# Filter spectra of four chunks kept in SBUF over the end of a stage, and stored later from another queue

## The chip, the cores and the metric

The kernel runs on one core of one Trainium2 chip (trn2). The metric is the device time of one execution in microseconds, the median over several executions. The engines are TensorE (PE, with PEld for its weight loads), VectorE (DVE), ScalarE (ACT) and GpSimd (POOL). SyncE (SP) issues most of the DMAs and ACT some of them. The 16 DMA engines carry both queues.

## What is computed

A long convolution by FFT, gated by its input, and then an MLP with two matrices, over 2 batches of 12480 tokens of 128 values:

```python
h_filt = (np.maximum(pos_emb @ w1, 0.0) @ w2) * window
u = x * v
Uf = np.fft.rfft(u, n=L, axis=1)
Hf = np.fft.rfft(h_filt, n=L, axis=0)
y = np.fft.irfft(Uf * Hf[None, :, :], n=L, axis=1)[:, :S, :]
attn_out = x * y
h = attn_out.reshape(B * S, D) @ w_in
out = np.maximum(0.01 * h, h) @ w_out
```

The filter's spectrum `Hf` is the same for both batches.

## The kernel before

**Stages.** The transforms are done as matrix products. In the first stage, 16 chunks of rows of batch 0 are loaded, multiplied (`x*v`), transformed and stored to DRAM (`scr1`), together with the filter's rows. The second stage (the loop over `ORD`, from line 823) takes 25 chunks of 4 frequencies. Of each it makes the filter's spectrum `hs` (PE line 846, ACT copies line 850), the input's spectrum `up` (line 135), their complex product on DVE and POOL (`product`, lines 143 and 144), and the way back `dp` (line 163), which ACT copies to `ct` (line 238). After the stage tile 0 of batch 0 is joined and gated (`front0`), and then the MLP runs in blocks of up to 512 tokens with 16 steps each (`m1`, `m2`, lines 1009 and 1050 to 1052). It is fed by `front(t)` for tiles of 390 tokens, and batch 1's convolution (`conv`) is done in pieces between the MLP's steps.

**What is stored.** `hspec` in DRAM holds the filter's spectrum for batch 1: `store_h` (line 809) issues two DMAs of 256 KB for each chunk on ACT's queue. Batch 1 reads it back at line 489, some 250 us later. `ct` goes to `scr2`, one chunk behind, also from ACT's queue (`store_back`, line 220). The weights' conversion (`weights`, lines 708 to 762) is spread over the same loop: DVE turns 64-bit data into 32-bit, in eight parts whose loads (lines 717, 718) SP issues.

**Order.** Each engine executes its instructions in the order in which the program writes them, and waits only by semaphores. The SP queue in the loop holds, in this order: the chunk three ahead (`load_b`, line 705), parts of tile 0's upper rows (`first_c`), in chunks 20 and 23 a whole input chunk of batch 1's first stage (`fetch_a`: one load of `ft` and six of `x` and `v`), in chunks 23 and 24 the gating data of tiles 0 and 1 (`load_gx`). Behind the loop come the last rows of tile 0 (`last_c`, line 657), the last `store_back`, the rows of tile 1 (`upper_c(1)` and `rows_c`, lines 629 to 650), and the loads of tile 2. In the MLP a list of steps (`at(i, what, t)`, carried out by `do`) says at which step a load is issued or a piece done. Step 2 has "piece" (stores held back and the third `fetch_a`), step 6 the loads of tile 3 ("loadc"), step 9 the third product `mult_a` on POOL and tile 3's gating data ("loadg"), steps 13 and 14 tile 4's loads, steps 16 to 23 the sums of tile 3 on POOL (`join_hi`, `join_lo`: tiles `cq` and `cp`), step 25 the transform of tile 3 on PE (`yp`, line 932). Batch 1's chunk 2 issues the fourth `fetch_a` at its beginning, and between its two halves the fourth `mult_a` stands in POOL's queue, ahead of the last `cp` of tile 3.

**Buffers.** `fetch_a` takes its three tiles from pool `s0`, tags `s0` (3 buffers), `s1` (3) and `s2` (2), in rotation. The two first fetches are made in the second stage, the third at MLP step 2. The results `o1` of batch 1's first stage rotate over two buffers of tag `s4` in pool `sc`. `hs` has two buffers of its own. The first `next(conv)`, which stands ahead of the loop, runs only to the first `yield`: it takes the first `o1` buffer and issues nothing.

Of the kernel before, what the change touches and what calls it, by code (L numbers as in the profile page):

```python
# [8 lines left out]
F32 = mybir.dt.float32  # L9
# [12 lines left out]
MC1 = 4  # L22
KC = 4
# [7 lines left out]
def tile_conv_mlp(ctx, tc, x, v, pos_emb, w1, w2, w_in, w_out, cf, cr, cg, cb, ci, cw, out):  # L31
# [210 lines left out]
    with tc.manual_schedule():  # L242
# [175 lines left out]
        wc_l = wp.tile([128, D], F32R, name="wc_l")  # L418
        sc = ctx.enter_context(tc.tile_pool(name="sc", bufs=2, reuse_waits="tile"))
        psc = {}  # L420
        N1 = HB // MC1
        WAIT = 12
        PRE = 2
# [273 lines left out]
        with ExitStack() as st:  # L697
# [97 lines left out]
            def evac(c):  # L795
# [10 lines left out]
                    last_c(ct, k0, n, [nc.sync] * 3 + [nc.scalar if end else nc.sync])  # L806
                store_back(0, c, ct, nc.sync if end else nc.scalar)

            def store_h(c, hs, i):

                w = chunk(c)[1] * D

                def put(eng):
                    for s in range(2):
                        eng.dma_start(out=hspec[c][:, :, s, :w], in_=hs[HB * s:HB * s + HB, :, :w])
                put(nc.scalar)

            eh, dps = {}, {}
            first_c = upper_c(0)
            ahead(A0)  # L820
            next(conv)
            hidden(ORD[0])
            for i, c in enumerate(ORD):
                if i + 3 < NCH:
# [18 lines left out]
                for ri in range(2):  # L843
                    for k in range(n):
                        h, j = 64 * (k % 2), ri * n // 2 + k // 2
                        nc.tensor.matmul(hp[k % 2][:, D * j:D * j + D], es[h:h + 64, k // 2, ri, :], w22[h:h + 64, :],
                                         start=True, stop=True)
                hs = sbb.tile([128, 2, KC // 2, 2, D], F32, tag="hs", name="hs", bufs=2)
                for k in range(2):
                    nc.scalar.copy(hs[:, :, :n // 2, k, :],  # L850
                                   hp[k][:, :n * D].rearrange("p (r j d) -> p r j d", r=2, d=D))
# [28 lines left out]
            back_halves(dps[ORD[-1]], pins.pop(ORD[-1]), ORD[-1])  # L880
            evac(ORD[-1])
            run(join_hi(0))
            run(upper_c(1))
            rows_c(1, 0, 0, KH)
            psc["held"] = []
# [278 lines left out]
                at(0, "load", t)  # L1164

        at(2, "piece", 0)
        at(9, "mult", PRE)

        def do(what, t, i):
            if what == "piece":  # L1170
                run(pieces_out.pop(0))
                for f in psc.pop("held"):
                    f()
                fetch_a(PRE)
            elif what == "mult":
                mult_a(t)
            elif what == "conv":
                run(conv)
                load_tile(t)
                load_tile(t + 1)  # L1180
            elif what == "load":
                if t not in ld:
                    load_tile(t)
            elif what == "loadc":
                load_c(t)
            elif what == "loadg":
                load_gx(t)
            elif what == "join":
                run(join(t))
            elif what == "sum":  # L1190
                if t not in joins:
                    joins[t] = join(t)
                next(joins[t])
            elif t in fronts:
                next(fronts[t], None)
            else:
                fronts[t] = front(t, i // NF)
                next(fronts[t])
# [118 lines left out]
```

## Time and profile before

| | us |
|---|---|
| median of 3 runs | 1598.55 |
| lowest, highest | 1595.64, 1606.63 |
| profiled execution | 1601.6 |
| its span, first to last instruction | 1599.7 |
| PE busy | 1555.3 (97%) |
| DVE, ACT, POOL busy | 1138.7, 998.1, 767.0 |

The page's table of 40 slices of 40 us each gives the stages: the first up to about 140 us, the second up to about 315, then the MLP. The DMA engines are busy for eight tenths and more up to 280 us, mostly for five to seven tenths up to some 960 us, where batch 1's convolution runs beside the MLP, and for two tenths or less at the end. The granted TensorE clock is 0.996 of full speed over the span (full speed is 2.4 GHz, the lower level 1.2 GHz). In the rows below each engine's line says when an instruction began, how long it took, and in brackets how long the engine had idled ahead of it and what ended that. A line with "x2" is two instructions merged. SPq and ACTq are DMA issues and other queue instructions; their time is that of the issue, not of the transfer.

### The profile page before, as it was taken

What the parts mean: (1) busy time and instruction counts of PE and PEld (TensorE: products, weight loads), DVE (VectorE), ACT (ScalarE), POOL (GpSimd) and SP (SyncE); (2) the same over time, 40 slices, a digit from 0 to 9 for tenths busy, and PEclk for the clock granted to TensorE, in tenths of its full rate; (3) what the DMA queues carried; (4) which work ended last, traced back from release to release, by engine and by line L of the source; (5) the groups of instructions that cost most, each with busy time, mean ns of one, the idle gap of its engine ahead of it and who ended that gap; (6) DMA issues with size and microseconds to landing.
All of it is one profiled execution on the core that took longest, in us unless ns stands there. A gap on an engine that the chain in (4) does not pass through costs nothing.

```text
span 1599.7 us, 27485 instructions
## 1 busy us (share of the span) xinstructions
PE 1555.3 (97%) x9241; PEld 1322.6 (83%) x9241; DVE 1138.7 (71%) x1785; ACT 998.1 (62%) x2108; POOL 767.0 (48%) x806
## 2 busy tenths in 40 slices
PE   7888999899999999999999999999999999999998
PEld 7887555588889888888888888988888888888888
DVE  6874888756975566666676765677777777777776
ACT  2332555346664477777777776667777676777776
POOL 6772122146654275867776873633443433334310
PEclk9999999999999999999999999999999999999999
DMA  9998999767767477657556650421212212121200
GB/s 268 304 307 283 320 318 340 243 198 203 222 198 216 136 194 192 197 162 197 173 160 181 171 153 32 138 85 55 69 54 68 80 57 89 56 61 59 64 11 21
DMA packets 166268, 253.30 MB, mean 158 GB/s; under 512 B 14240, under 2 KB 118932, under 8 KB 163056
## 3 DMA queue, kind: packets, MB, share of 16 engines
q1 hardware_dynamic: 146388, 226.28, 47.7%
q10 hardware_dynamic: 19740, 25.28, 4.5%
q8 instruction: 73, 1.20, 0.3%
q14 instruction: 67, 0.55, 0.1%
HBM read 168.03 MB, written 83.43 MB: 157 GB/s over the span
## 4 chain that ended last, share of the span: by engine, by line
PE 75%; DMA 11%; DVE 8%; ACT 2%; issue 2%; POOL 1%; SPq 1%; ACTq 0%; DVEq 0%; POOLq 0%
PE mh L1009 29%; PE acc L1051 9%; PE acc L1052 9%; PE acc L1050 9%; PE yp L932 4%; PE cv L149 3%; DMA scr<-o 3%; PE cv L445 3%; DMA scr<-ct 2%; DMA ft<-in_cf_dram 2%; PE op L1082 2%; PE a L398 2%; PE zp L951 1%; PE up L135 1%; DVE ta L143 1%
## 5 line engine op out<-in xcount | busy, mean ns | idle before, releaser
L1014 DVE SCALAR_TENSOR_TENSOR rl<-mh,rh 128x512 fp32r<-128x512 f32 (+1 forms) x336 | 226.7, 682 | 198.7 <-ACT rh L1013 197.4
L1022 DVE TENSOR_TENSOR rl<-mh,rh 128x512 fp32r<-128x512 f32 (+2 forms) x416 | 277.4, 670 | 83.6 <-ACT rh L1021 75.1
L1017 ACT ACTIVATE mh<-mh 128x512 f32<-128x512 f32 (+2 forms) x416 | 236.9, 570 | 153.8 <-PE mh L1009 143.5
L1009 PE MATMUL mh<-zh,w_in_h 128*128 128x512 f32 (+3 forms) x800 | 315.9, 395 | 3.8 <-DVE rl L1014 2.6
L1009 PE MATMUL mh<-zl,w_in_h 128*128 128x512 f32 (+3 forms) x800 | 299.2, 374 | 0.3 <-POOL zl L965 0.2
L1051 PE MATMUL acc<-rl,w_out_h 128*128 128x512 f32 (+3 forms) x800 | 299.1, 374 | 0.1
L1050 PE MATMUL acc<-rh,w_out_h 128*128 128x512 f32 (+3 forms) x800 | 299.0, 374 | 0.0
L1052 PE MATMUL acc<-rh,w_out_l 128*128 128x512 f32 (+3 forms) x800 | 299.0, 374 | 0.0
L1009 PE MATMUL mh<-zh,w_in_l 128*128 128x512 f32 (+3 forms) x800 | 299.0, 374 | 0.0
L1013 ACT ACTIVATE rh<-mh 128x512 fp32r<-128x512 f32 (+1 forms) x336 | 199.1, 596 | 136.8 <-PE mh L1009 128.4
L965 POOL TENSOR_TENSOR zl<-zf,zh 128x390 fp32r<-128x390 f32 (+24 forms) x110 | 67.7, 628 | 395.7 <-ACT zh L964 371.0
L687 POOL TENSOR_TENSOR cp<-cq,cp 98x256 f32<-98x256 f32 x248 | 194.1, 783 | 29.3 <-DVE cp L675 12.6
L1019 DVE CAST rh<-mh 128x512 fp32r<-128x512 f32 (+2 forms) x208 | 139.5, 671 | 65.6 <-ACT mh L1017 65.3
L1009 PEld LDWEIGHTS mh<-zh,w_in_h 128*128 128x128 f32 x800 | 151.2, 189 | 30.1 <-DVE rl L1014 9.2
L1051 PEld LDWEIGHTS acc<-rl,w_out_h 128*128 128x128 f32 x800 | 151.2, 189 | 20.2 <-DVE rl L1022 0.4
L1050 PEld LDWEIGHTS acc<-rh,w_out_h 128*128 128x128 f32 x800 | 151.2, 189 | 19.8
L1052 PEld LDWEIGHTS acc<-rh,w_out_l 128*128 128x128 f32 x800 | 151.2, 189 | 19.7
L1009 PEld LDWEIGHTS mh<-zh,w_in_l 128*128 128x128 f32 x800 | 151.2, 189 | 19.7
L1009 PEld LDWEIGHTS mh<-zl,w_in_h 128*128 128x128 f32 x800 | 151.6, 190 | 15.9 <-POOL zl L965 0.6
L1021 ACT CAST rh<-mh 128x512 fp32r<-128x512 f32 (+2 forms) x208 | 118.7, 571 | 6.7
L684 POOL TENSOR_TENSOR cq<-cin 98x256 f32<-98x256 f32 x124 | 97.3, 784 | 0.9 <-DMA cin<-scr 0.8
L144 POOL TENSOR_TENSOR pin<-ta,tb 128x512 f32<-128x512 f32 (+1 forms) x23 | 28.8, 1253 | 130.7 <-DVE tb L143 130.7
(168 smaller groups left out, 2559.3 us busy)
## 6 DMA issues: line engine op xcount, KB each, us to landing
cin<-scr SPq DMA_DIRECT2D x318, 98.0 KB
hd<-hspec SPq DMA_DIRECT2D x48, 512.0 KB
bin<-scr SPq DMA_DIRECT2D x24, 768.0 KB
scr<-o SPq DMA_DIRECT2D x28, 588.0 KB
scr<-ct SPq DMA_DIRECT2D x25, 512.0 KB
scr1b<-o SPq DMA_DIRECT2D x32, 392.0 KB
hspec<-hs ACTq DMA_DIRECT2D x48, 256.0 KB
xm<-in_x_dram SPq DMA_DIRECT2D x128, 96.0 KB
```

Of the source, the lines that this page charges most:

```text
L684: eng.tensor_tensor(out=cq[:, p], in0=ci_t[:, 0, :, 0, :], in1=ci_t[:, 0, :, 1, :], op=op)
L687: eng.tensor_tensor(out=cp[:, p, w], in0=cq[:, p], in1=cp[:, p, 1], op=op)
L1009: nc.tensor.matmul(hp, u[:, fs], m, start=(i == 0), stop=(i == 2))
L1013: nc.scalar.activation(out=split2(rh), in_=plain(hp), func=AF.Relu)
L1014: nc.vector.scalar_tensor_tensor(out=split2(rl), in0=plain(hp), scalar=0.0, in1=split2(rh), op0=ALU.max, op1=ALU.subtract)
L1017: nc.scalar.activation(out=hp, in_=hp, func=AF.Lrelu, alpha=0.01)
L1019: nc.vector.tensor_copy(split2(rh), plain(hp))
L1021: nc.scalar.copy(split2(rh), plain(hp))
L1022: nc.vector.tensor_tensor(out=split2(rl), in0=plain(hp), in1=split2(rh), op=ALU.subtract)
L1050: nc.tensor.matmul(ap, w_out_h[:, f, :], rh, start=(f == 0 and not sums(k)), stop=False)
L1051: nc.tensor.matmul(ap, w_out_h[:, f, :], rl, start=False, stop=False)
L1052: nc.tensor.matmul(ap, w_out_l[:, f, :], rh, start=False, stop=(f == NF - 1))
```

## The change

For the chunks at places 19 to 22 of the order, `hs` is not written to its own two buffers but to other ones: two share one buffer of tag `s4`, one takes a buffer of tag `s1`, one of tag `s0`. The stores to `hspec` are not issued in the loop from ACT but kept as functions that issue them from SP: the first two (four DMAs) behind the stage ahead of tile 1's loads, the third and fourth (two DMAs each) at MLP steps 6 and 7, where step 6 already has the loads of tile 3 ahead of it. The first `next(conv)` moves from ahead of the loop to chunk 19, behind the allocation of the shared buffer, so that this buffer comes first in the rotation and the first `o1` second. What is computed is the same.

```diff
--- before.py
+++ after.py
@@ -418,6 +418,7 @@
         wc_l = wp.tile([128, D], F32R, name="wc_l")
         sc = ctx.enter_context(tc.tile_pool(name="sc", bufs=2, reuse_waits="tile"))
         psc = {}
+        kept = []
         N1 = HB // MC1
         WAIT = 12
         PRE = 2
@@ -806,6 +807,25 @@
                     last_c(ct, k0, n, [nc.sync] * 3 + [nc.scalar if end else nc.sync])
                 store_back(0, c, ct, nc.sync if end else nc.scalar)
 
+            KEEP = range(NCH - 6, NCH - 2)
+            pair = []
+
+            def place_h(i):
+
+                j = i - KEEP[0]
+                if i not in KEEP:
+                    return sbb.tile([128, 2, KC // 2, 2, D], F32, tag="hs", name="hs", bufs=2)
+                if j < 2:
+                    if j == 0:
+                        pair.append(sc.tile([128, 2048], F32, tag="s4", name="hs2"))
+                        next(conv)
+                    t = pair[0][:, 1024 * j:1024 * j + 1024]
+                elif j == 2:
+                    t = s0.tile([128, 1024], F32, tag="s1", name="hs1", bufs=3)
+                else:
+                    t = s0.tile([128, MC1 * 4 * NA], F32, tag="s0", name="hs0", bufs=3)[:, :1024]
+                return t.rearrange("p (r j i d) -> p r j i d", r=2, j=KC // 2, d=D)
+
             def store_h(c, hs, i):
 
                 w = chunk(c)[1] * D
@@ -813,12 +833,13 @@
                 def put(eng):
                     for s in range(2):
                         eng.dma_start(out=hspec[c][:, :, s, :w], in_=hs[HB * s:HB * s + HB, :, :w])
-                put(nc.scalar)
+                if i in KEEP:
+                    kept.append(lambda: put(nc.sync))
+                else:
+                    put(nc.scalar)
 
             eh, dps = {}, {}
             first_c = upper_c(0)
-            ahead(A0)
-            next(conv)
             hidden(ORD[0])
             for i, c in enumerate(ORD):
                 if i + 3 < NCH:
@@ -845,7 +866,7 @@
                         h, j = 64 * (k % 2), ri * n // 2 + k // 2
                         nc.tensor.matmul(hp[k % 2][:, D * j:D * j + D], es[h:h + 64, k // 2, ri, :], w22[h:h + 64, :],
                                          start=True, stop=True)
-                hs = sbb.tile([128, 2, KC // 2, 2, D], F32, tag="hs", name="hs", bufs=2)
+                hs = place_h(i)
                 for k in range(2):
                     nc.scalar.copy(hs[:, :, :n // 2, k, :],
                                    hp[k][:, :n * D].rearrange("p (r j d) -> p r j d", r=2, d=D))
@@ -880,6 +901,8 @@
             back_halves(dps[ORD[-1]], pins.pop(ORD[-1]), ORD[-1])
             evac(ORD[-1])
             run(join_hi(0))
+            for f in kept[:2]:
+                f()
             run(upper_c(1))
             rows_c(1, 0, 0, KH)
             psc["held"] = []
@@ -1164,6 +1187,8 @@
                 at(0, "load", t)
 
         at(2, "piece", 0)
+        at(6, "kept", 2)
+        at(7, "kept", 3)
         at(9, "mult", PRE)
 
         def do(what, t, i):
@@ -1172,6 +1197,8 @@
                 for f in psc.pop("held"):
                     f()
                 fetch_a(PRE)
+            elif what == "kept":
+                kept[t]()
             elif what == "mult":
                 mult_a(t)
             elif what == "conv":
```

## Rows read from the trace of the kernel before

**Rows 1.** Chain of waits, middle of the stage: start us, us, engine, tile, line

```profile
186.57 0.69 DVE ta L143
...
192.30 0.68 DVE ta L143
...
198.40 0.68 DVE ta L143
...
204.81 0.68 DVE ta L143
```

**Rows 2.** Windows: us, busy (instructions) by engine, then PEclk, DMA share, GB/s

```profile
core 0: us, PE busy (x) PEld busy (x) DVE busy (x) ACT busy (x) POOL busy (x), PEclk, DMA share, GB/s
264.00:270.00 6.00, 6.00 (x52) 3.51 (x52) 5.58 (x13) 2.53 (x6) 1.28 (x1) 1.00 1.01 351
295.00:300.00 5.00, 5.00 (x28) 2.33 (x30) 4.76 (x8) 2.35 (x5) 3.36 (x2) 0.70 0.96 291
318.00:324.00 6.00, 4.64 (x35) 3.02 (x34) 3.95 (x12) 0.69 (x4) 1.46 (x2) 1.00 0.54 177
```

**Rows 3.** Chain of waits, end of the stage

```profile
281.40 8.61 DMA scr<-ct
```

**Rows 4.** Timeline of ACT, end of the stage

```profile
291.73 1.07 ACT L850 COPY hs<-hp 128x512 f32<-128x512 f32 x2 [5.41 <-DVE fb L90]
...
303.90 1.07 ACT L238 COPY ct<-dp 128x512 f32<-128x512 f32 x2 [4.04 <-DMA hspec<-hs]
```

**Rows 5.** Timeline of DVE, the first product of chunks 19, 21, 22 and 23

```profile
270.52 0.68 DVE L143 TENSOR_TENSOR ta<-up,hs 128x512 f32<-128x512 f32 x1
...
284.03 0.69 DVE L143 TENSOR_TENSOR ta<-up,hs 128x512 f32<-128x512 f32 x1 [0.42 <-ACT hs L850]
...
292.90 0.69 DVE L143 TENSOR_TENSOR ta<-up,hs 128x512 f32<-128x512 f32 x1 [1.14 <-ACT hs L850]
...
301.46 0.68 DVE L143 TENSOR_TENSOR ta<-up,hs 128x512 f32<-128x512 f32 x1
```

**Rows 6.** Line 734 from 255 us (ns min/median/max), and POOL beside its last

```profile
L734 DVE TENSOR_TENSOR w_in_l<-wi,w_in_h x3: 411/426/2383, 255.5 to 296.3; 128x256 fp32r<-128x256 f32 x3
...
295.56 2.80 POOL L262 TENSOR_TENSOR xv<-xv,xv 98x1024 f32<-98x1024 f32 x1
```

**Rows 7.** Issues of hspec's stores and loads: ns min/median/max, first and last start

```profile
L815 ACTq DMA_DIRECT2D hspec<-hs x50: 515/516/1186, 156.6 to 308.1; - x50
L489 SPq DMA_DIRECT2D hd<-hspec x50: 451/578/610, 558.0 to 953.1; - x50
```

**Rows 8.** Timeline of PE and DVE, the MLP's first steps

```profile
323.10 0.43 PE L1009 MATMUL mh<-zh,w_in_h 128*128 128x390 f32 x1 [0.70 <-ACT zh L996]
...
326.31 0.42 DVE L684 TENSOR_TENSOR cq<-cin 98x256 f32<-98x256 f32 x1
...
327.18 0.69 DVE L100 TENSOR_TENSOR o<-cv,a1s 98x512 f32<-98x512 f32 x1
```

**Rows 9.** Timeline of SP: tile 1's first loads, and the fourth fetch's first

```profile
316.93 1.48 SPq L629 DMA_DIRECT2D cin<-scr  x3
...
350.88 0.33 SPq L249 DMA_DIRECT2D ft<-in_cf_dram  x1
```

**Rows 10.** Waits of SP, 240 to 345: us in total, times, longest

```profile
SPq L650 <- DMA cin<-scr: 1.3, 2, 1.1
```

**Rows 11.** Timelines of POOL and PE around tile 3's transform

```profile
359.20 2.36 POOL L262 TENSOR_TENSOR xv<-xv,xv 98x1024 f32<-98x1024 f32 x1 [9.61 <-DMA xv<-in_v_dram]
361.51 0.74 POOL L687 TENSOR_TENSOR cp<-cq,cp 98x256 f32<-98x256 f32 x1
...
362.80 1.10 PE L932 MATMUL yp<-cp,gt 98*64 98x128 f32 x16
```

**Rows 12.** Timeline of PE in the stage, after two stops

```profile
293.35 1.16 PE L846 MATMUL hp<-w,es 64*128 64x128 f32 x16 [2.55 <-ACT es L793]
294.93 3.44 PE L135 MATMUL up<-bin,mb 128*64 128x512 f32 x8 [0.42 <-DVE ta L143]
...
304.22 1.94 PE L135 MATMUL up<-bin,mb 128*64 128x512 f32 x8 [1.59 <-DVE ta L143]
```

## The prediction, made before the result

> **What bounds the kernel now.** I read the page first (engines and slices), then the chain of waits from 140 to 420 us, then three timelines (ACT, SP, DVE) around the place that the diff touches. From the page the reader takes that PE is busy 97% of the span, and that all but a short early part is the MLP: what is won ahead of the MLP is worth its full size, and what is lost in it too. The change sits at the end of batch 0's second stage and in the first MLP blocks, so only 260 to 370 us need a close look.
>
> The stage has two limits that nearly coincide. DVE: in the undisturbed middle, the first product instruction of every third chunk comes 18.24 us later [rows 1], that is 6.08 us a chunk, in steps of 5.73, 6.10 and 6.41 us that repeat. DMA: the windows show a busy share of 1.01 at 351 GB/s shortly before the end of the stage [rows 2], so a chunk's traffic fills its time. At chunk 20 the loop adds seven loads for the first conversion chunk of batch 1, at chunk 23 seven more, and there the DMA side gives way. The chain leaves the engines and runs along a `ct` store of 8.61 us [rows 3]. The reader is to see in ACT's timeline what that costs: ACT issues these stores itself, and an issue is held until an earlier transfer has landed, so the copies behind it stand. `hs` of chunk 22 is written after 5.41 us of idling, `ct` of chunk 22 after 4.04 us that the trace puts down to a `hspec` store [rows 4].
>
> How much of this reaches the end is read from DVE, which does the products in order [rows 5]. From chunk 19 at 270.52, the undisturbed steps would put chunk 20 at 276.93 (+6.41), 21 at 282.66 (+5.73), 22 at 288.76 (+6.10). The last two come at 284.03 and 292.90: 1.4 and 4.1 us late, and both wait for ACT's `hs`. From 22 to 23 it takes 8.56 instead of 6.41, but that is not the DMAs: one `w_in_l` of 2.38 us, where its median is 0.43 [rows 6], runs beside POOL's 2.80 us product of the next stage, 1.96 us of the 2.15. So the DMA congestion costs the stage **4.1 us**, and some 0.2 more behind.
>
> **The change part by part.**
> *Eight stores leave ACT's queue* (chunks 19 to 22, two each of 256 KB). Issue time is 0.52 us each [rows 7], 1.0 us a chunk on ACT, which is not what holds DVE when nothing is blocked: nothing. What counts is 8 x 262 kB = 2.1 MB out of the crowded window: at 351 GB/s, 6.0 us of transfer time. The loads of chunk 20 and the weights that DVE converts then land earlier, and the waits of `hs` for its two-buffer ring (chunk 21 for the stores of 19, 22 for 20, 23 for 21) are gone. Bounds: below, nothing, if the loads fill the freed time; above, the 4.3 us, and 2 x 1.96 more if both POOL products (the second follows in the tail) came to lie beside instructions that they do not hold. Since 6.0 us of relief is more than the 4.1 us of lag, and the late products waited for just these copies, I take **-4.1 us**.
> *`next(conv)` moves to chunk 19*: it only allocates, it issues nothing on any queue. Nothing. The pair's buffer then goes to the second `o1`, first written by DVE at 327.18 [rows 8]; the two stores from it are issued some 8 us earlier. Hidden; if they landed later, DVE and all `rl` behind it would stand.
> *The two idle `s0`/`s1` buffers*: the third `fetch_a` now takes chunk 0's buffers and the fourth the kept ones. Chunk 0 is read before the MLP begins, and between the kept stores and the fourth fetch SP issues all of tile 4's loads. Nothing.
> *Four store issues on SP behind the last `store_back`.* SP issues a transfer of this shape in 0.58 us (the loads of `hspec` [rows 7]), so 2.1 to 2.3 us stand ahead of the seven `cin` loads of tile 1, which start at 316.93 now [rows 9]. Cover: SP itself waits up to 1.1 us for an earlier transfer ahead of the last two of these loads [rows 10], the DMA share is 0.54 there [rows 2], and DVE's `cq`, which needs them, starts at 326.31 [rows 8], over 5 us after the last issue. I take nothing for `cq`, and a shift of 1.0 to 2.3 us for everything behind on SP.
> *Four more at steps 6 and 7.* They stand behind tile 3's `cin` loads and ahead of tile 3's and 4's remaining loads and of the fourth `fetch_a`, which SP issues from 350.88 [rows 9]: again 2.1 to 2.3 us. From here nothing is free. SP goes from load to load, and the fourth fetch is awaited: POOL idles 9.61 us for it, multiplies 359.20 to 361.56, then does the last `cp` of tile 3 until 362.25, and PE transforms tile 3 at 362.80 [rows 11]. The slack is at most 0.55 us. A later fetch makes a later `mult_a(3)`, a later `cp`, and a PE that stands, with all MLP matmuls behind it.
> So SP is late by 2.1 us (the first four absorbed) to 4.6 (none absorbed). I take 3.1, the first four costing 1.0 net of the wait that they fill. Less 0.4 of slack: **+2.7 us** of idle PE; below, zero, if the fetch were not bound by its issue; above 4.6.
> *The clock.* After 2.55 us of idle PE the matmuls `up` took 3.44 us; after 1.59 us of idle they took 1.94 [rows 12], and the granted clock in that first stretch is 0.70 [rows 2], so part of it ran at the lower level (1.2 GHz). In the stage this hid behind DVE. In the MLP PE is the bound, and a stop of 2.7 us is nearer the first row: 3.44 - 1.94 = **+1.5 us**; zero if the stop stays under some 1.6 us.
> Sum: -4.1 + 2.7 + 1.5 = +0.1 us, on the profiled execution's span of 1599.7 us (1601.6 around it, 1.9 us outside). The median of the runs shown is 1598.55; the same sum there gives 1598.7.
>
> The rows give the issue of such a transfer (0.58 us [rows 7]) and not what stands behind it on its queue. Against the move to SP speaks a rule of the Trainium skill, "DMA: Bandwidth & Descriptors", section "Queues, rings and completion order": SP and ACT each own one ring on every DMA engine, and a ring is consumed in order. By it a load behind four stores on SP waits for their data, not just for their issue: an estimate of 1.05 MB / 351 GB/s = 3.0 us in place of my 2.1, and no run yet shows which. By the issue alone the sum stands at +0.1, by the rule at some +1 us.
>
> **The rivals.**
> (a) *The gain stays*: SP's shift is swallowed, because the waits of SP for landings, not its issues, set the fourth fetch. For it: SP's waits [rows 10]. Against: POOL's 9.61 us wait ends 0.55 us before PE. Then -4.1: 1594.4.
> (b) *Slower*: the deferred stores hold the ring and SP longer than the issues say. The place is the same, tile 3's `cp`. It decides from a shift of SP of 3.0 us on (3.0 - 0.4 + 1.5 = 4.1, the gain). With both groups of stores waiting for their data, 2 x 3.0 = 6.0: 5.6 of stop, 1.5 of clock, less 4.1 gives +3.0: 1601.5. For it: each group is 1.05 MB, 3.0 us at 351 GB/s [rows 2]; against: the DMA share is 0.54 where the first group falls. The rule named above would make it so.
> (c) *The change brings nothing in the stage*: the loads of chunk 20, not the stores, hold ACT. For it: ACT's queue is held by whatever landed late, and the store rows of [rows 3] are `ct`, which stay. Against: 6.0 us of 2.1 MB. Then 0 + 2.7 + 1.5: 1602.8.
>
> **How the numbers follow.** Forecast (gain and new stop cancel, within 2.5 us): 0.40. (a) 0.25, (b) 0.20, (c) 0.10, something else 0.05. Time: 1598.7, own range 1596 to 1601. The range to 1592 takes in (a) with one POOL product also unhidden from DVE (1594.4 - 2.0 = 1592.4), the one to 1605 takes in (b), (c) and some 2 us above them. All cases lie within 1%, or 16 us, which is about what a measurement of this kernel can tell from no change: faster 0.02, same 0.95, slower 0.03.
>
> **What would show it.** Gain: the first products of chunks 20 to 23 step by 5.73, 6.10 and then some 8.4 us; no ACT copy idles over 2 us for a store; the first MLP matmul, at 323.10 now [rows 8], starts near 319. Loss: POOL's idling ahead of the fourth `mult_a` relative to the first MLP matmul; PE idle some 3 us ahead of tile 3's `yp`, granted clock under 1 behind it. Wrong if the first MLP matmul does not move, if `yp` of tile 3 does not wait, or if DVE stands at `cq` of tile 1 or at the second `o1`.

## The result, and the profile after

The changed kernel takes 1610.09 us (median of 10 runs, 1606.5 to 1617.36), the kernel before 1599.53 us (10 runs in the same session). The ratio is 1.0072, 95% interval 1.0051 to 1.0093: about 11 us slower, where +0.1 us was forecast; it lies within 1%, as most of the chance said, and outside the range of 1592 to 1605. The interval is 0.2% to either side, so the loss is clear of chance; the prediction had taken 1% for what a measurement can tell. The profiled execution of after has a span of 1605.7 us at a mean granted clock of 0.994, the one of before 1599.7 us at 0.996.

The first look is at the stage, where 4.1 us were to be won. All positions below are taken against the first product of chunk 19, since what lies ahead of it is the same in both programs and differs only from execution to execution (that product starts between 264.6 and 274.0 us in the sixteen profiles of this case). The timeline of DVE in the kernel after, the first product instructions of chunks 19, 22, 23 and 24, with what stands between them (start, us, engine, line, operation; in brackets the idle time ahead and its releaser):

```profile
265.31 0.68 DVE L143 TENSOR_TENSOR ta<-up,hs 128x512 f32<-128x512 f32 x1
...
281.96 0.29 DVE L80 TENSOR_SCALAR fa<-wi 128x256 uint32<-128x256 uint32 x1 [1.25 <-DMA wi<-in_moe_w_in_dram]
...
284.87 0.68 DVE L143 TENSOR_TENSOR ta<-up,hs 128x512 f32<-128x512 f32 x1
...
288.04 2.58 DVE L735 TENSOR_TENSOR w_in_l<-wi,w_in_h 128x256 fp32r<-128x256 f32 x1
...
292.18 2.46 DVE L88 TENSOR_TENSOR fa<-fb,fs 128x256 uint32<-128x256 uint32 x1
...
295.48 0.68 DVE L143 TENSOR_TENSOR ta<-up,hs 128x512 f32<-128x512 f32 x1
...
303.08 0.29 DVE L759 SCALAR_TENSOR_TENSOR wcs<-wcp,wcs 128x128 f32<-128x128 f32 x1 [3.34 <-PE wcp L754]
303.29 0.68 DVE L143 TENSOR_TENSOR ta<-up,hs 128x512 f32<-128x512 f32 x1
```

From chunk 19 to 22 it takes 19.56 us, before 22.38 [rows 5]: 2.8 us are won, and no product waits for ACT's `hs` any more. From 22 to 23 it takes 10.61 us instead of 8.56, from 23 to 24 7.81 instead of 6.36 (the first product of chunk 24 stood at 307.82 before). Two instructions between 22 and 23 are six times as long as their kind, and both lie beside POOL. The timeline of POOL in the kernel after:

```profile
287.52 2.81 POOL L262 TENSOR_TENSOR xv<-xv,xv 98x1024 f32<-98x1024 f32 x1
291.91 2.44 POOL L262 TENSOR_TENSOR xv<-xv,xv 98x1024 f32<-98x1024 f32 x1 [1.58 <-DMA gt<-in_cg_dram]
```

Before, only the first of the two ran between these two products of DVE [rows 6]; the second began one chunk later, once its fetch had landed. The timelines of POOL and DVE in the kernel before:

```profile
304.45 2.37 POOL L262 TENSOR_TENSOR xv<-xv,xv 98x1024 f32<-98x1024 f32 x1 [6.09 <-DMA xv<-in_v_dram]
304.70 2.66 DVE L144 TENSOR_TENSOR pin<-ta,tb 128x512 f32<-128x512 f32 x1
...
307.82 0.68 DVE L143 TENSOR_TENSOR ta<-up,hs 128x512 f32<-128x512 f32 x1
```

It stretched an instruction there too, `pin` to 2.66 us (0.69 otherwise), but most of that was hidden: from chunk 23 to 24 it takes 6.36 us here and 5.58 in e4_mult below, where nothing is stretched in that chunk and DVE waits 1.10 us for PE instead. In the emptier DMA window the second product starts 7.3 us earlier against chunk 19, and now falls into the same chunk as the first. PE, which waits for DVE's product meanwhile, stands for 5.14 us, and then runs slowly. The timeline of PE, and the windows of the same place (us, busy by engine with instruction counts, PEclk, DMA share, GB/s), in the kernel after:

```profile
298.23 3.68 PE L135 MATMUL up<-bin,mb 128*64 128x512 f32 x8 [5.14 <-DVE ta L143]
301.84 1.21 PE L754 MATMUL wcp<-wo,wts 128*128 128x128 f32 x4
...
318.57 0.43 PE L1032 MATMUL mh<-zh,w_in_h 128*128 128x390 f32 x1 [0.70 <-ACT zh L1019]
```

```profile
296.00:300.00 4.00, 1.77 (x6) 0.62 (x8) 3.67 (x7) 1.38 (x4) 0.00 (x0) 0.51 0.41 109
300.00:304.00 4.00, 4.00 (x16) 1.72 (x14) 0.92 (x3) 0.00 (x0) 0.00 (x0) 0.64 0.23 71
```

The same eight matmuls `up` took 1.94 us in chunk 24 before [rows 12]. This time DVE waits for them, 3.34 us at `wcs`. With that the first MLP matmul, at 318.57, comes 0.7 us *later* against chunk 19 than before [rows 8]. DMA is no longer the limit here: its share is 0.41 and 0.23, where it was 0.83 and 0.72 in the same two slices of before, counted from chunk 19 (301.2 to 309.2 us).

The second look is at the MLP's first tiles. The timelines of SP, DVE and PE around tile 1, and of SP, POOL and PE around tile 3, in the kernel after:

```profile
312.40 3.56 SPq L835 DMA_DIRECT2D hspec<-hs  x4
316.00 2.18 SPq L630 DMA_DIRECT2D cin<-scr  x3
...
323.70 0.43 DVE L685 TENSOR_TENSOR cq<-cin 98x256 f32<-98x256 f32 x1 [1.82 <-DMA cin<-scr]
...
326.71 0.65 PE L955 MATMUL yp<-cp,gt 98*64 98x128 f32 x6 [1.56 <-DVE cp L688]
```

```profile
339.97 3.10 SPq L835 DMA_DIRECT2D hspec<-hs  x4
...
353.01 0.32 SPq L249 DMA_DIRECT2D ft<-in_cf_dram  x1
...
361.33 2.34 POOL L262 TENSOR_TENSOR xv<-xv,xv 98x1024 f32<-98x1024 f32 x1 [13.52 <-DMA xv<-in_v_dram]
363.63 0.72 POOL L688 TENSOR_TENSOR cp<-cq,cp 98x256 f32<-98x256 f32 x1
...
360.19 0.87 PE L955 MATMUL yp<-cp,gt 98*64 98x128 f32 x10
364.41 1.11 PE L955 MATMUL yp<-cp,gt 98*64 98x128 f32 x6 [3.35 <-POOL cp L688]
365.45 0.80 PE L1032 MATMUL mh<-zh,w_in_h 128*128 128x512 f32 x1
366.04 0.63 PE L1032 MATMUL mh<-zl,w_in_h 128*128 128x512 f32 x1
```

The first four issues take 3.56 us and the second four 3.10, together 6.66 us; each is longer than the 0.58 us at which they had been priced. Tile 1's loads are issued that much later against the end of the stage, `cq` waits 1.82 us for them and PE 1.56 us at `yp`; at tile 3 PE waits 3.35 us for POOL's `cp`, and the matmuls behind take 0.80 and 0.63 us instead of 0.38 for 2.3 us. The window of that place (the granted clock, third from the end, is 0.57):

```profile
364.00:368.00 4.00, 3.59 (x13) 2.76 (x14) 1.46 (x3) 0.60 (x1) 0.35 (x1) 0.57 0.51 169
```

The account of the two profiles, against chunk 19 and in us (a second profile of after, from the first experiment, in brackets):

| from, to | forecast | measured |
|---|---|---|
| chunk 19 to first product of chunk 22 | -4.1 | -2.8 (-3.7) |
| chunk 22 to first MLP matmul | 0 | +3.5 (+2.6) |
| tile 1's transform | 0 | +1.9 (+3.3) |
| tile 3: stop of PE, and its clock | +4.2 | +5.4 (+5.4) |
| first load of the second batch's second stage, near 569 us | 0 | +1.6 (+1.6) |
| the rest | 0 | +1.6 (+1.3) |
| sum | +0.1 | +11.2 (+10.5) |

The span of after is only 6.0 us longer than that of before, since its chunk 19 came 5.2 us earlier. Of the +3.3 in brackets 1.7 are slow matmuls behind the stop. "The rest" is no measured cost of the change: the second profile of before has +1.3 there too.

### The profile page after: what moved, and what is told of

Read it like the earlier page. It is cut to its first block, busy times and chain, and to the rows that moved or that the text cites. A ratio compares the mean times of both kernels' runs of the same rounds, so it can differ in the third digit from the quotient of the medians.

```text
span 1605.7 us, 27481 instructions
## 1 busy us (share of the span) xinstructions
PE 1557.7 (97%) x9241; PEld 1325.0 (83%) x9241; DVE 1141.9 (71%) x1785; ACT 996.9 (62%) x2108; POOL 765.5 (48%) x806
## 4 chain that ended last, share of the span: by engine, by line
PE 73%; DMA 10%; DVE 9%; ACT 2%; issue 2%; POOL 1%; SPq 1%; ACTq 0%; DVEq 0%; POOLq 0%
PE mh L1032 28%; PE acc L1074 9%; PE acc L1073 9%; PE acc L1075 9%; PE yp L955 4%; PE cv L149 3%; DMA scr<-o 3%; PE cv L446 3%; DMA ft<-in_cf_dram 2%; PE op L1105 2%; DMA scr<-ct 2%; PE zp L974 1%; PE up L135 1%; DVE ta L143 1%; PE a L398 1%
## 5 line engine op out<-in xcount | busy, mean ns | idle before, releaser
L688 POOL TENSOR_TENSOR cp<-cq,cp 98x256 f32<-98x256 f32 x248 | 193.4, 780 | 30.8 <-DVE cp L676 14.1
L676 POOL TENSOR_TENSOR cp<-cin 98x256 f32<-98x256 f32 x78 | 57.7, 759 | 69.9 <-DVE rl L1037 26.6
```

The lines of the kernel that those rows point to most:

```text
L688: eng.tensor_tensor(out=cp[:, p, w], in0=cq[:, p], in1=cp[:, p, 1], op=op)
```

## The experiments

A number given as a ratio is against the kernel before in the same session. "Stage" is the time from chunk 19's first product to the first MLP matmul, "tiles" that from there to the 100th MLP matmul, which lies behind tile 3; both are the profile's, less those of the first profile of before. The table gathers them; the runs are told one by one below.

| run | stores deferred, by | `mult_a(0)` at chunk | stage | tiles | time: ratio, interval |
|---|---|---|---|---|---|
| before, profiled again | none | 23 | -2.3 | 0.0 | 1.0004 (0.9985 to 1.0023) |
| e8_base_mult | none | 22 | +0.8 | +0.9 | 0.9993 (0.998 to 1.0007) |
| after | eight, SP | 23 | +0.7 | +7.3 | 1.0072 (1.0051 to 1.0093) |
| e1_again | eight, SP | 23 | -1.1 | +8.8 | 1.0057 (1.0038 to 1.0076) |
| e4_mult | eight, SP | 22 | -2.8 | +8.6 | 1.0045 (1.0027 to 1.0062) |
| e2_act | eight, ACT | 23 | +0.3 | +6.1 | 1.0021 (1.0007 to 1.0035) |
| e9_pool | eight, POOL | 22 | -1.7 | +1.3 | 1.0013 (0.9998 to 1.0029) |
| e3_late | eight, SP, steps 62 to 65 | 23 | +0.6 | 0.0 | 1.0025 (1.0012 to 1.0038) |
| e11_late_mult | eight, SP, steps 62 to 65 | 22 | -4.0 | 0.0 | 1.0021 (1.0005 to 1.0036) |
| e7_in24 | eight, ACT, in the last chunk | 22 | +2.8 | 0.0 | 1.0005 (0.9982 to 1.0028) |
| e5_first | first four, SP | 23 | +0.6 | +2.7 | 1.0005 (0.9986 to 1.0025) |
| e10_first_mult | first four, SP | 22 | -4.3 | +3.2 | 1.0003 (0.9987 to 1.0018) |
| e13_behind | first four, SP, behind tile 1's loads | 22 | -1.9 | +4.6 | 0.9988 (0.9975 to 1.0) |
| e12_first_pool | first four, POOL | 22 | -0.7 | 0.0 | 1.0005 (0.9989 to 1.002) |
| e6_second | second four, SP | 23 | +2.3 | +1.6 | 1.0035 (1.0012 to 1.0058) |

**The two kernels once more.** base_again and e1_again carry no edit.

> The kernel before once more, for a second profile, so that stops of PE late in the MLP (1.8 us at batch 1's second stage's first matmul near 565 us, 1.4 us near 631, which the changed kernel and most variants show and the first profile of before does not) can be put down to the change or not. Theory A: some of these are chance, this profile shows one of them at least, and the PE stops at tiles 1 and 3 stay under 0.6 us. Rival: neither appears, and they are a cost of the change.

> The changed kernel once more, for a second profile. Theory A (the stores stand in SP's queue ahead of loads that PE needs: PE stops of 1.9 us at tile 1 and of 5.4 us at tile 3 with the low clock behind it; in the stage both POOL products fall into chunk 23): the same stops at the same places, in all +10 us against before. Rival (the profiled execution was a chance one, and the loss lies elsewhere, for example in the first load of batch 1's second stage): the stops at tiles 1 and 3 differ by more than 1 us from 1.9 and 5.4.

The stage of before came 2.3 us apart in two profiles, so a difference of that size in "stage" between two single profiles says nothing. The column "tiles" is steadier: 0.0 in both profiles of before, +7.3 and +8.8 in those of after. e1_again's tile 1 is 1.4 us off its expectation: the stop there is 1.33 us, but the matmuls behind it run at the lower level (granted clock 0.50 in 334 to 336 us), which they did not behind after's stop of 1.56. base_again also has a stop of PE of 1.66 us at 633 us (`cv`, waiting for ACT's `ct`); after has one of 1.49 us there, so that one isn't the change's.

**The stores from ACT, at the same places.**

```
...
-                    kept.append(lambda: put(nc.sync))
+                    kept.append(lambda: put(nc.scalar))
...
```

> All eight deferred stores are issued from ACT's queue at the same places instead of SP's. Theory A (position in SP's queue): tile 1's and tile 3's loads no longer stand behind them, both stops go, -7.3 us against the changed kernel, some +3 us against before. Rival B (the 2.1 MB themselves compete with the loads, whoever issues them): the stops stay, +9 to +11 us against before. Rival C (ACT's issue time in the MLP, 0.5 us each, is what PE then waits for): tile 3 free, but PE waits for rh at steps 6 and 7, some +1 us each.

The time falls to +3.4 us over before, some two thirds of the loss gone, but "tiles" only to +6.1: the stops are smaller at tiles 1 and 3 and a new one stands at tile 2; theory A had the time, not the stops. The timelines of ACT and PE in this kernel:

```profile
310.31 5.47 ACTq L835 DMA_DIRECT2D hspec<-hs  x4
...
344.64 0.48 PE L1032 MATMUL mh<-zl,w_in_h 128*128 128x512 f32 x1 [2.64 <-POOL zl L988]
...
363.66 0.65 PE L955 MATMUL yp<-cp,gt 98*64 98x128 f32 x6 [1.06 <-POOL cp L688]
```

Four issues hold ACT 5.47 us, longer than SP. The low clock behind tile 3 does not occur: the stop there is 1.06 us. So the place of the stores on SP is part of the harm, and the stores near these tiles cost something on either queue.

**The stores later, from other data.** The stores read the weights instead of `hs`, so the four chunks' spectra are not written.

```
...
-            for f in kept[:2]:
-                f()
...
-        at(6, "kept", 2)
-        at(7, "kept", 3)
+        for j in range(4):
+            at(62 + j, "kept", j)
...
```

> The eight stores go from the stage and the MLP's first blocks to steps 62 to 65, from SP, with other data (the weights) as their source, so batch 1's spectra of these four chunks are not computed. It shows the stage's part alone. Theory A: no stop at tiles 1 and 3, -7.3 us against the changed kernel, +3 us against before, and the stage itself as in the changed kernel (no gain by its end). Rival B (competition by transfers) expects the same here. Rival D (the buffers' new rotation delays the fetches): the stop at tile 3 stays, +8 us or more against before.

"Tiles" falls to 0.0 exactly: without stores at these two places tiles 1 and 3 stand where they stood before. So the whole +7 to +9 us there belongs to the deferred stores. The time stays at +4 us, since the stores delay a fetch in their new place too; the timelines of SP and PE there:

```profile
444.40 4.92 SPq L840 DMA_DIRECT2D hspec<-w_in_h  x6
...
466.58 1.12 PE L446 MATMUL cv<-xv,ft 98*98 98x128 f32 x8 [1.46 <-DVE o L102]
```

The stage is no faster than before in this kernel, which leaves the other half of the loss to explain.

**POOL's product one chunk earlier.**

```
...
-                if i == NCH - 2:
+                if i == NCH - 3:
                     mult_a(0)
...
```

> The changed kernel with the first POOL product of the next stage one chunk earlier (chunk 22). Theory A (two products in chunk 23 hold DVE 2.0 us each, PE idles 5.1 us and runs its next matmuls at the lower level of its clock): one product leaves chunk 23, PE idles 3 us or less there, the first MLP matmul is 2 to 3.5 us earlier, +7 to +8.5 us against before. Rival (the stage is late for another reason): no change in the first MLP matmul, +10 us.

The timelines of POOL, DVE and PE in this kernel:

```profile
284.11 2.82 POOL L262 TENSOR_TENSOR xv<-xv,xv 98x1024 f32<-98x1024 f32 x1
295.23 2.35 POOL L262 TENSOR_TENSOR xv<-xv,xv 98x1024 f32<-98x1024 f32 x1 [2.83 <-DMA gt<-in_cg_dram]
...
292.87 0.41 DVE L735 TENSOR_TENSOR w_in_l<-wi,w_in_h 128x256 fp32r<-128x256 f32 x1
294.85 0.43 DVE L88 TENSOR_TENSOR fa<-fb,fs 128x256 uint32<-128x256 uint32 x1
295.31 2.55 DVE L90 SCALAR_TENSOR_TENSOR fb<-wo,fs 128x256 f32<-128x256 uint32 x1
...
300.99 1.94 PE L135 MATMUL up<-bin,mb 128*64 128x512 f32 x8 [1.39 <-DVE ta L143]
```

The first product now lies between chunks 21 and 22, beside an instruction for whose load DVE had waited 0.78 us anyway (`fa<-wi`, line 80: 1.59 us instead of 0.29; that step takes 8.26 us, in after 7.43). Between 22 and 23 only the second is left: DVE's two instructions are back at 0.41 and 0.43 us, and it stretches the next one, to 2.55. So the step takes 8.53 us instead of 10.61, PE stands 1.39 us instead of 5.14, `up` is back at 1.94, and the stage comes out 2.8 us under before, 3.5 under after. Chunks 22 to 24 take 17.5 to 18.5 us in the five profiles with both products in one chunk (after, e1_again, e2_act, e3_late, e6_second), and 14.1 to 14.9 in this one and the two of before. That is the hand-back of the stage, shown by taking its cause away. "Tiles" stays at +8.6, and the time is 1.0045.

**The same early product in the kernel before.** The edit alone, without any kept chunk.

> The kernel before with one edit alone: the first product of the next stage's head (mult_a(0)) is asked for at chunk 22 of the loop instead of chunk 23. Theory A (in the kernel before the product waits for its fetch, which lands only behind chunk 22, so the place in the program does not set it): POOL's two products stay near 295.6 and 304.5 us of that profile's scale, the first MLP matmul stays within the 2.3 us by which this stage varies from execution to execution, and the time is that of before within 2 us. Theory B (the earlier place alone is worth what the changed kernel with this edit won in the stage, some 3.4 us, whatever the stores do): the first MLP matmul comes about 3 us earlier against chunk 19, and the time is 3 us less, since nothing behind the stage is touched.

The place in the program does set it, which theory A denied: POOL's first product starts at 285.67 us, ahead of chunk 22's, and chunk 23 starts 3.8 us earlier than before against chunk 19. But the DMAs take that back by the first MLP matmul (+0.8); a window and the timeline of ACT in this kernel:

```profile
296.00:300.00 4.00, 3.46 (x28) 1.88 (x26) 3.86 (x9) 0.58 (x1) 0.00 (x0) 1.00 1.05 369
```

```profile
301.94 1.07 ACT L238 COPY ct<-dp 128x512 f32<-128x512 f32 x2 [5.24 <-DMA hspec<-hs]
```

ACT stands 5.24 us behind a store while the DMA share is 1.05, the congestion that the change relieves. The time is that of before. Its "tiles" of +0.9 is no stop: the MLP's first matmuls take 0.53 us instead of 0.33 (granted clock 0.50 in 326 to 328 us), behind the same 0.70 us of idling as in before. So do those of e4_mult, the timeline of PE there:

```profile
321.20 0.53 PE L1032 MATMUL mh<-zh,w_in_h 128*128 128x390 f32 x1
```

The earlier product and the relief are each worth nothing alone; in the profiles with both (but for e7_in24, below) the stage comes out 0.7 to 4.3 us shorter than in the first profile of before, and in the mean 0.2 us shorter than in its second.

**Half the change, each half.** In e5_first only chunks 19 and 20 are kept (`KEEP = range(NCH - 6, NCH - 4)`, no stores at steps 6 and 7), in e6_second only 21 and 22 (`KEEP = range(NCH - 4, NCH - 2)`, no stores behind the stage).

> Chunks 19 and 20 alone are kept and stored from SP behind the stage; 21 and 22 are stored from ACT in the loop as before. Theory A: a stop of some 1.9 us at tile 1; at tile 3 SP is late by what the first group leaves, 1 to 2 us with 1.9 of it absorbed by PE's own lateness, so a stop under 1 us and no low clock; +3 to +4 us against before. Rival (the two groups act only together): under +1 us.

> Chunks 21 and 22 alone are kept and stored from SP at steps 6 and 7; 19 and 20 are stored from ACT in the loop as before. Theory A: no stop at tile 1; at tile 3 SP is late by these four issues, some 3 us, a stop of 2.5 to 3 us and 1.5 us of low clock: +4 to +5 us against before, the stage itself unchanged to 1 us. Rival (the first group sets both stops): no stop over 1 us at tile 3.

The first four stores alone make the stop at tile 1; the timeline of PE in e5_first:

```profile
329.21 0.66 PE L955 MATMUL yp<-cp,gt 98*64 98x128 f32 x6 [1.48 <-DVE cp L688]
```

The second four alone make one at tile 3 and none at tile 1; the timeline of PE in e6_second:

```profile
369.03 0.66 PE L954 MATMUL yp<-cp,gt 98*64 98x128 f32 x6 [1.19 <-POOL cp L688]
```

That is 1.19 us where 2.5 to 3 were expected, and no low clock follows. So neither half makes the 3.35 us: they add up on SP, 3.56 and 3.10 us. e5_first's time is not measurably over before, where +3 to +4 us were expected; e6_second's is, by 5.8 us, of which its profile has 1.6 in "tiles" and 2.3 in the stage, a difference that says nothing by itself. The clock of all executions says more: the mean granted clock is 0.9917 in after, 0.9920 in e1_again, 0.9925 in e4_mult, 0.9920 in e6_second and 0.9928 in e2_act, against 0.9940 to 0.9946 of before and 0.9936 to 0.9953 of the kernels without stores at steps 6 and 7 from SP or ACT. An estimate from these: at 1600 us, 0.0025 is 4 us of full clock, of which the single profile of after (0.994 against 0.996) shows some 3. No profile shows where the other executions lose it, so that these stores lower the clock beyond tile 3 is not shown.

**All eight stores in the last chunk.** The four chunks' stores are issued by ACT in the last chunk of the loop, with the early product.

> The changed kernel with the eight stores issued from ACT in the loop's last chunk, where the changed kernel's DMA share is 0.51 and less and ACT idles 7.6 us, and with the first POOL product one chunk earlier. Theory A: the stage keeps its gain (first MLP matmul 2.8 us early), no stop at tiles 1 and 3: -2 to -3 us against before. Rival B (2.1 MB cost their time wherever they go): the tail's loads of tile 0 come late, first MLP matmul no earlier than before, 0 to +3 us.

"Tiles" is 0.0, and the stage pays: the timeline of ACT and a window of this kernel:

```profile
305.87 8.61 ACTq L835 DMA_DIRECT2D hspec<-hs  x10
314.52 1.07 ACT L238 COPY ct<-dp 128x512 f32<-128x512 f32 x2 [8.68 <-DMA hspec<-hs]
```

```profile
308.00:312.00 4.00, 3.37 (x24) 2.17 (x20) 3.63 (x6) 0.00 (x0) 0.00 (x0) 1.00 1.00 321
```

Ten issues, the eight and the last chunk's own two, hold ACT 8.61 us while the DMA share is 1.00 at 321 GB/s, and the last `ct` stands behind them. The stage had 2.9 us in hand at chunk 24 and ends 2.8 late.

**The stores from POOL.** As e4_mult, with `put(nc.gpsimd)` for the kept chunks.

> The changed kernel with two edits: mult_a(0) at chunk 22 (as in the run of that edit alone, 1.0045 of before), and the eight deferred stores issued by POOL at the same two places, so that neither SP's nor ACT's queue holds them. Theory A (SP's queue is the harm: tile 1's and tile 3's loads stand behind the stores on it): no stop of PE over 0.5 us at tiles 1 and 3, no low clock behind tile 3, the stage's gain of 2.8 us stays up to mh100, and the time is 2 to 3 us under before, but for chance at the second batch. Theory B (2.1 MB cost their time wherever they are issued, or POOL's own queue is held by them as ACT's was): POOL's cp of tile 1 or its third product stand behind the held issues, PE stops 1 us or more at tile 1, 2 or 3, and the time is 3 us or more above before.

The timelines of POOL and PE in this kernel:

```profile
294.53 2.47 POOL L835 DMA_DIRECT2D hspec<-hs  x4
...
360.18 0.66 PE L955 MATMUL yp<-cp,gt 98*64 98x128 f32 x6 [0.92 <-POOL cp L688]
```

"Tiles" falls from +8.6 to +1.3 with the same bytes at the same two places of the program. POOL reaches the first of them earlier, behind its last product, so the stores' time moved as well as their queue. Theory A nearly held for the stops (0.92 us is left at tile 3), but not for the time: 1.0013, 2 us over before in the median, though this profile's span is 2.5 us under it.

**Half the change and the early product; then the same stores behind tile 1's loads; then from POOL.** e10_first_mult is e5_first with `mult_a(0)` at chunk 22. e13_behind moves its stores:

```
...
-            for f in kept[:2]:
-                f()
             run(upper_c(1))
             rows_c(1, 0, 0, KH)
+            for f in kept[:2]:
+                f()
...
```

> Only chunks 19 and 20 are kept (four stores, from SP behind the stage; none at steps 6 and 7), and mult_a(0) stands at chunk 22. Theory A (costs and gains add: the half change cost 1.8 at tile 1 and 0.9 at tile 3 and won nothing at the first MLP matmul, +0.6; the earlier product won 3.4 there): first MLP matmul 2.5 to 3 us earlier than before against chunk 19, at mh100 0 to -1 us, time 1 to 2 us under the kernel of that half change, so some 1 us under before. Theory B (the half relief brings the fetch too late for the earlier place): the products stay where they were in the half change and the time is that of it, 1.000 of before.

> Chunks 19 and 20 kept, mult_a(0) at chunk 22, and the four deferred stores issued by SP as in the changed kernel, but behind tile 1's loads instead of ahead of them. Theory A (tile 1's stop is the order on SP: its loads stand behind the four stores): PE's stop of 1.4 us at tile 1's yp is gone, and tile 2's loads, now behind the stores, have the slack to stay without a stop; mh100 3 us earlier than before against chunk 19. Theory B (the 1.05 MB of the stores take the transfers' time wherever they stand near tile 1): the stop stays at 1 us or more, at tile 1 or at the second o1, whose buffer the stores must leave, or at tile 2.

> Chunks 19 and 20 kept, mult_a(0) at chunk 22, and the four deferred stores issued by POOL instead of SP (none at steps 6 and 7). Theory A (the same kernel with SP's stores won 4.3 us up to the first MLP matmul and lost 3.2 of them at tile 1 and its joins): without SP's stores no stop over 0.5 us at tile 1, mh100 is 3 to 4 us earlier than before against chunk 19, and the time is 2 to 3 us under before. Theory B (the stage's gain in a single profile is for the most part chance, since the kernel before itself came 2.3 us apart in two profiles; its mean is under 2 us): the time is within 1.5 us of before.

The timeline of PE in e10_first_mult, then that of SP and PE in e13_behind:

```profile
328.46 0.65 PE L955 MATMUL yp<-cp,gt 98*64 98x128 f32 x6 [1.43 <-DVE cp L688]
...
332.20 0.53 PE L1032 MATMUL mh<-zh,w_in_h 128*128 128x390 f32 x1
```

```profile
315.82 3.42 SPq L835 DMA_DIRECT2D hspec<-hs  x4
...
324.87 0.65 PE L955 MATMUL yp<-cp,gt 98*64 98x128 f32 x6 [0.58 <-DVE cp L688]
...
342.81 0.48 PE L1032 MATMUL mh<-zl,w_in_h 128*128 128x512 f32 x1 [1.28 <-POOL zl L988]
...
362.47 0.65 PE L955 MATMUL yp<-cp,gt 98*64 98x128 f32 x6 [1.71 <-POOL cp L688]
```

Behind tile 1's loads, on the same queue, the stop of 1.43 us falls to 0.58, and what PE has lost when it ends from 1.8 to 0.9 us: half of tile 1's loss was the order on SP, not the transfer as such. (Of e10_first_mult's +3.2 in "tiles" the other 1.5 us are slow matmuls behind the stop, 0.53 us instead of 0.33.) The 3.42 us of issue do not vanish; they make the third and the fourth fetch late, and PE stops for them at 342.81 and 362.47; where a gain of 3 us at the 100th matmul was expected, the profile has a loss of 2.7. From POOL there is nothing left at the tiles ("tiles" 0.0), but the 100th matmul comes 0.7 us earlier instead of 3 to 4, and the time is that of before, as theory B said. The times, 1.0003, 0.9988 and 1.0005, all hold 1 within their intervals or touch it.

**Late stores and the early product.** e3_late with `mult_a(0)` at chunk 22.

> The changed kernel with the deferred stores put at steps 62 to 65 of the MLP from other data (the second batch's spectra of four chunks are therefore not those of the reference, and the four chunks' spectra are not written), and mult_a(0) at chunk 22: both suspected causes taken away at once. Theory A (the stage's gain is real and only the POOL product and the stores near tiles 1 and 3 took it back): first MLP matmul and mh100 both 2.5 to 3 us earlier than before against chunk 19, and the time 3 us under that of the run with late stores alone (1.0025 of before), so within 1 us of before; what stays of that run's +4 is stops near the stores' new place. Theory B (something else at tiles 1 to 3 takes any gain back, since the MLP's start is bound by loads): mh100 stays at +0.5 as with late stores alone, and so does the time.

In the profile both gains add up as theory A says: -4.0 in the stage, 0.0 in the tiles, 3.9 us still in hand at the 100th MLP matmul (1.6 against the second profile of before). The time doesn't follow (1.0021, 1.2 us less over its session's before than e3_late, where 3 were expected): some 5 us go again behind the late stores, in stops as large as 1.89 us.

## Why the prediction was wrong

*The relief in the stage.* The mechanism was right, and its size at chunk 22 was -2.8 instead of -4.1 (-1.3 against the second profile of before): a wait of 1.25 us for a weight load stayed. The waits for ACT's `hs` went, as said.

*The gain kept up to the MLP: the step that failed first.* The prediction priced the two POOL products only as a gain that might come on top ("2 x 1.96 more if both came to lie beside instructions that they do not hold"). It did not ask what the earlier fetch does to the second one. It moved out of a chunk in which most of its 2 us was hidden into one that DVE bounds: +2.0 us, with PE idle for 5.14 us and `up` at 3.68 instead of 1.94 behind it, for which DVE waits in turn, +1.45. Of -2.8 nothing was left. e4_mult, which moves the first product, undoes it. In the time nothing of it was seen: no kernel with the stage's gain is measurably faster than before.

*The first four stores, taken at nothing for tile 1: the step that failed second.* The cover named was SP's own wait of up to 1.1 us [rows 10] and 5 us of slack of `cq`. Measured: +1.9 us at tile 1, +1.8 with those four stores alone, and half of it gone with the stores behind tile 1's loads. The slack was counted from the issue of the loads; `cq` waits for them to land, and the shift was 3.56 us where 1.0 to 2.3 were allowed. DVE standing at `cq` of tile 1, 1.82 us here, was one of the prediction's own signs of being wrong.

*Tile 3.* Place, queue and releaser were right: the fourth fetch, POOL's `cp`, PE's `yp`. The term mis-sized is SP's lateness. It was taken as 3.1 us, with part of the first group absorbed; the issues measured 3.56 + 3.10 = 6.66, and nothing was absorbed: against the first MLP matmul POOL's product ends 6.6 us later (45.1 us behind it instead of 38.5 [rows 8, 11]). PE had itself lost 1.9 at tile 1, and has 0.55 us of slack and the 0.87 us of the ten matmuls that it may do first: 6.6 - 1.9 - 1.4 = 3.3, where 3.35 was measured and 2.7 forecast. Of what is left of the 5.4 us, 1.6 is the slow matmuls, for 1.5 forecast: from the end of the stop to the 100th MLP matmul it takes 15.24 us, in e6_second and e13_behind, whose clock stays full, 13.66. The other 0.4 comes with any such stop (1.62 us lost for 1.19 of stop in e6_second). That the size came out right was luck, for [rows 12] had been read by the stop's length alone: behind 1.33 and 1.43 us at tile 1 the clock fell (e1_again, e10_first_mult), behind 1.71 at tile 3 it did not (e13_behind). The price per issue, 0.58 us from [rows 7], came from loads on a quiet queue; here it is 0.83 in the mean (0.59 to 1.09). This is rival (b), slower, in place and mechanism, with its condition met (SP late by over 3.0 us); its time, 1601.5, lacked the two steps above. The lateness of 6.6 us is the issue time alone: against the first MLP matmul SP issues the fourth fetch's first load 6.66 us later [rows 8, 9], and POOL's product begins 8.32 us behind that issue in both profiles. For tile 1 the landing was not told apart. The prediction's rule from the Trainium skill, "DMA: Bandwidth & Descriptors", section "Queues, rings and completion order", spoke for this side, and the order on SP decided half of the loss at tile 1 (e13_behind). The fourth fetch, some 10 us behind the last store on the same queue, waited no longer for its data than before; whether tile 1's loads, right behind the stores, waited for the stores' data on their ring no run here shows.

*What was left out.* The first load of the second batch's second stage: PE waits 1.34 us near 569 us for `tl`, which stands behind ACT's `th`, which waits for a `bin` load. The timelines of ACT and PE in the kernel after:

```profile
566.79 0.62 ACT L499 CAST th<-bin 128x512 fp32r<-128x512 f32 x1 [1.80 <-DMA bin<-scr1b]
...
569.28 0.48 PE L149 MATMUL cv<-tl,mb_h 128*128 128x512 f32 x1 [1.34 <-DVE tl L504]
```

From the issue of that load to `th` it takes 5.83 us, before 4.32. The stop is in the profile of every kernel in which SP issues all eight stores (after, e1, e3, e4, e11) and in none of the other eleven. Why the number of earlier issues on SP should matter there was not settled. Nor was it why kernels whose profile shows 3 to 4 us won by the 100th MLP matmul are not faster in the median, but 2.3 us of that is the choice of the first profile of before as the measure; a single profile places a loss well, but here it sizes a difference only to 2 or 3 us.

## What to carry to other kernels

Before pricing a relief, ask what arrives earlier because of it, and beside which instructions that work will then run: here a fetch by which POOL's product came 7 us earlier put that product into the chunk that DVE bounds and took back all that the DMAs had given. A store deferred to a queue that feeds the next stage costs its queue more than its quiet issue time (0.83 us instead of 0.58 here), and everything behind it on that queue can be late by the whole sum. Put behind the loads that are awaited next, the stores moved the stop to the next fetches ("tiles" +4.6); from a queue that had nothing to feed there, POOL's, they cost 0.0 and +1.3. Two edits that are each worth nothing (the earlier product, the relief) may be worth something together, though no time here shows it, so an experiment that undoes one part at a time needs its counterpart on the kernel before.

## What the runs showed of the hardware

An issue is not a fixed price: the same store took 0.52 us on ACT in the stage [rows 7], 0.72 to 1.00 on SP behind the stage, 0.56, 0.83, 1.74 and 2.23 in the four that follow each other on ACT in e2_act, and ten of them 8.61 us on ACT while the DMA share was 1.00. What stands behind it on that engine, compute included, waits as long (`ct` 8.68 us in e7_in24).

A POOL product of 98x1024 stretches a DVE instruction with two operands in SBUF beside it from 0.42 to 2.46 or 2.58 us, integer operations included, and in e9_pool one with a single operand (`fa<-wi`, line 80) from 0.29 to 2.46. The Trainium skill, "SBUF — State Buffer", section "Terms", says that VectorE and GpSimd lock a pair of ports that they share for a whole instruction, and that the loser stands meanwhile; the traces agree, with 2.0 to 2.2 us lost to each of these hits (less where DVE's instruction began in the middle of the product).

The granted clock fell to its lower level (1.2 GHz) in part of 296 to 304 us behind a stop of 5.14 us (0.51 and 0.64 in the two windows), and behind the 3.35 us at tile 3 (0.57 in 364 to 368 us). The length of the one stop ahead of it does not tell when: behind stops of 0.92 to 1.71 us at tile 3 in other kernels no slow matmuls followed, nor behind 1.48 and 1.56 us at tile 1 (e5_first, after), but behind 1.33 and 1.43 us at tile 1 they did (e1_again, e10_first_mult), and at the MLP's beginning behind 0.70 us in e4_mult and e8_base_mult, where the other profiles have 0.70 to 0.89 us and full clock.
